# A fused attention and squared-ReLU MLP kernel: one written order for all five engines in place of a scheduled plan

## The chip, the cores and the metric

The kernel runs on one core of a Trainium2 chip. The metric is the device time of one execution in microseconds (us). Three runs of the kernel before gave 272.69 to 273.59 us, with a median of 273.18 us.

## The reference

There are 8 batches (b) of 8 heads, 576 tokens and a head dimension of 64. A second small input `p` has 32 rows per batch and head. All inputs are float32.

```
def sm_attn(qq, kk, vv):                       # softmax attention, scale 1/8
    s = scale * matmul(qq, kk.T); s = s - max(s)
    a = exp(s); a = a / (sum(a) + 1e-9)
    return matmul(a, vv)
p_packed = sm_attn(p, k, v)                    # 32 rows look at 576 tokens
out      = sm_attn(q, p_packed, p_packed)      # 576 tokens look at 32 rows
x = out as (8*576 tokens) x (8 heads*64)       # 4608 x 512
h = x @ w_in                                   # 512 -> 2048
y = square(max(h, 0)) @ w_out                  # 2048 -> 512
```

## The kernel before

**Units.** The heads are taken four at a time (`qd` = 0 or 1), so that 4 heads x 32 rows of `p` fill 128 partitions. For each of the 16 pairs (batch, `qd`) there is an attention chain, written as small steps named `st_...`:

- `st_k`, `st_q` (L170, L176): VectorE turns the loaded `k_b`, `q_b` into `kT`, `qT` in 32x32 blocks.
- `st_s1` (L183): first scores, 4 matmuls of 128x288 against a block-diagonal `pbd`, which VectorE builds (L110). Then `st_max1` (L193) and `st_exp1` (L198).
- `st_e1T` (L217): 6 transposes on TensorE; `st_e1T_out` evicts them; `st_pv` (L229): 24 small matmuls; `st_pp` scales; `st_bd` builds the second block-diagonal `bd`; `st_ppT` (L253).
- `st_s2` (L183): second scores, again 4 matmuls; then `st_turn2` (L265), `st_max2` (L269), `st_sub2` (L273), `st_exp2` (L278), `st_sum2` (L283), `st_a2` (L289), `st_a2T` (L296).
- `st_wp` (L305): the value product is folded into the MLP's first weights, `wp` = packed rows @ `w_in`, in two steps of 8 matmuls, with an eviction `wp<-ps_wp` (L309) each.

**The MLP.** Layer 1 of a batch makes `ps_h` = `wp` x `a2T`, 16 blocks of 128 features in two halves of 288 tokens, two matmuls each (L376; for batch 0 both halves at once, L393). ScalarE applies the ReLU into `r` (L379, L397), VectorE squares `r` into `gT` (L382, L402). Layer 2 makes 36 tiles of 128 tokens, `ps_o` += `gT` x `w_out_bf`, 16 matmuls of 128x512 each (L413). ScalarE evicts each tile into `o_sb` (L423), and four DMAs of 64 KB write it out (L429).

**What sets the order.** `first_batch` and `second_batch` are orders written out by hand for the engines; `busy` puts dummy matmuls (L159) between early steps. From there on `run` builds a plan: each unit of work gets a due time (batch number plus a fraction), for instance

```
at = (-0.12 if b > 2 else None, 0.02, 0.1, 0.18, 0.3, 0.38, 0.48, 0.6, 0.68)
plan.sort(key=lambda x: x[:2])
```

The sorted plan is TensorE's order; the tile scheduler places VectorE, ScalarE, GpSimd and the queues. Loads are issued from GpSimd's queue (`load1`, L129 and L132; `load_w_in`, L117; `load_w_out`, L122); outputs from SP's.

**PSUM.** Eight banks: two double-bank tiles `psa` for the attention steps, and two each of `psh` and `pso` for the MLP's two layers.

Of the kernel before, what the change touches and what calls it, by code (L numbers as in the profile page):

```python
# [17 lines left out]
POOL = mybir.EngineType.Pool  # L18

P = 128  # L20
D = 64
# [7 lines left out]
SCALE = 0.125  # L29


class Kernel:
# [10 lines left out]

    def __init__(self, tc, ctx, q, k, v, p, w_in, w_out, out):
        self.tc, self.nc = tc, tc.nc
        self.q, self.k, self.v, self.p = q, k, v, p
        self.w_in, self.w_out, self.out = w_in, w_out, out
        self.B, self.H = q.shape[0], q.shape[1]
        self.NQ = self.H // QH
        self.DM, self.DFF = w_in.shape  # L50
        self.NE = w_out.shape[1]
        self.NFB = self.DFF // P
        pool = lambda name, bufs: ctx.enter_context(tc.tile_pool(name=name, bufs=bufs))
        psum = lambda name, bufs: ctx.enter_context(
            tc.tile_pool(name=name, bufs=bufs, space=bass.MemoryType.PSUM))
        self.consts = pool("consts", 1)
        self.ld = pool("ld", 3)
        self.tp = pool("tp", 2)
        self.sm = pool("sm", 2)
        self.keep = pool("keep", 4)  # L60
        self.rp = pool("rp", 6)
        self.op = pool("op", 3)
        self.psa = psum("psa", 2)
        self.att = {}
        self.setup()

    def setup(self):
# [6 lines left out]
        make_identity(nc, self.ident)  # L74
# [12 lines left out]

        self.pT = self.consts.tile([P, G, 2 * NP], BF16, name="pT")
        self.pbd = self.consts.tile([P, G, QH, NP, 2], BF16, name="pbd")
# [4 lines left out]
    def p_cast(self):  # L94

        self.tc.keep_in_program_order(
            self.nc.vector.tensor_copy(self.p_b[:, :2 * self.NQ, :], self.p_f))

    def p_turn(self, g0, g1):
        self.tc.keep_in_program_order(  # L100
            self.nc.vector.transpose(self.pT[:, g0:g1, :].bitcast(U32), self.p_b[:, g0:g1, :].bitcast(U32)))

    def pack_diagonal(self, b):
        for g in range(b * self.NQ, (b + 1) * self.NQ):
            self.block_diagonal(self.pbd[:, g, :, :, :], self.pT[:, g, :])
# [8 lines left out]
    def load_w_in(self, c2):  # L114
        for c in range(2):
            f = c * (self.DFF // 2) + c2 * 512
            self.nc.gpsimd.dma_start(  # L117
                self.w_in_bf[c * D:(c + 1) * D, :, c2 * 512:(c2 + 1) * 512],
                self.w_in[:, f:f + 512].rearrange("(h d) f -> d h f", d=D))
# [5 lines left out]
    def load1(self, b, qd, n):  # L125
# [7 lines left out]
        self.att.setdefault((b, qd), {})[n] = x  # L133

    def load_behind(self, b):

        with self.tc.issue_after(self.last_pool):
            for n in "kvq":
                for qd in range(self.NQ):
                    self.load1(b, qd, n)  # L140
        with self.tc.issue_after(self.last_square):
            self.pack_diagonal(b)
# [9 lines left out]
    def psum(self, name, bufs):  # L152
        return self.tc.tile_pool(name=name, bufs=bufs, space=bass.MemoryType.PSUM)

    def busy(self, n):

        ps = self.idle.tile([P, 512], F32, name="ps_idle")
# [3 lines left out]
    def spare32(self, name):  # L161
        return self.spare.tile([P, 512], F32, name=name, tag="s")

    def spare16(self, name):
        return self.spare.tile([P, 1024], BF16, name=name, tag="s")
# [20 lines left out]

    def st_s1(self, t, g):
        t["ps_s1"] = self.turn32("ps_s1")
        self.scores(t["ps_s1"], self.pbd[:, g, :, :, :], t["kT"])
# [23 lines left out]
    def st_e1T(self, t, spare=False):  # L213
        nc = self.nc
        ps = (self.spare16("ps_e1T") if spare else self.turn16("ps_e1T")[:, 0, :])[:PS, :J * P].rearrange("p (j c) -> p j c", c=P)
        for j in range(J):
            nc.tensor.transpose(ps[:, j, :], t["e1"][:, j * PS:(j + 1) * PS], self.ident)  # L217
# [6 lines left out]
    def st_pv(self, t, spare=False):  # L224
        nc = self.nc
        ps = self.spare32("ps_pv")[:, :D] if spare else self.turn32("ps_pv")[:, 0, :D]
# [14 lines left out]
    def st_bd(self, t):  # L241
# [3 lines left out]
        nc.vector.transpose(x[:].bitcast(U32), t["pp"][:, 0, :].bitcast(U32))  # L245
        t["bd"] = self.tp.tile([P, QH, NP, 2], BF16, name="bd")
        self.block_diagonal(t["bd"][:], x[:])

    def st_ppT(self, t, spare=False):

        nc = self.nc
        ps = self.spare16("ps_ppT")[:, :P] if spare else self.turn16("ps_ppT")[:, 0, :P]
        nc.tensor.transpose(ps, t["pp"], self.ident)  # L253
        t["ppT"] = self.keep.tile([P, P], BF16, name="ppT")
        nc.scalar.copy(t["ppT"], ps)

    def st_s2(self, t):
        t["ps_s2"] = self.turn32("ps_s2")
        self.scores(t["ps_s2"], t["bd"][:], t["qT"])
# [16 lines left out]
    def st_exp2(self, t):  # L276
        t["e2"] = self.tp.tile([P, T, NP], F32, name="e2")
        self.nc.scalar.activation(t["e2"], t["d2"], ACT.Exp)  # L278
# [8 lines left out]
    def st_a2(self, t, engine):  # L287
        t["a2"] = self.tp.tile([P, T, NP], BF16, name="a2")
        ins = engine.tensor_tensor(out=t["a2"], in0=t["e2"], in1=t["rs"][:, :].unsqueeze(2).to_broadcast([P, T, NP]),  # L289
                                   op=ALU.mult)  # L290
        if engine is self.nc.gpsimd:
            self.last_pool = ins.ins

    def st_a2T(self, t):
        t["a2T"] = self.keep.tile([P, S], BF16, name="a2T")
        self.last_turn = self.nc.vector.transpose(t["a2T"], t["a2"][:].rearrange("p t i -> p (t i)")).ins  # L296

    def st_wp(self, t, qd, c2):
        nc = self.nc
        if c2 == 0:  # L300
            t["wp"] = self.keep.tile([P, 2, self.DFF // 2], BF16, name="wp")
        ps = self.turn32("ps_wp")
        for h in range(QH):
            for c in range(2):
                nc.tensor.matmul(ps[NP * h:NP * h + NP, c, :],  # L305
                                 lhsT=t["ppT"][D * c:D * c + D, NP * h:NP * h + NP],
                                 rhs=self.w_in_bf[D * c:D * c + D, QH * qd + h, c2 * 512:(c2 + 1) * 512],
                                 start=True, stop=True)
        nc.scalar.copy(t["wp"][:, :, c2 * 512:(c2 + 1) * 512], ps)  # L309

    def steps(self, b, qd):

        t, g = self.att[b, qd], b * self.NQ + qd

        dve = self.nc.vector

        pin = self.tc.keep_in_program_order if b < 4 else lambda ins: ins

        def k():
            pin(self.st_k(t))  # L320

        def s1():
            self.st_s1(t, g)
            self.st_max1(t)
            self.st_exp1(t)
            self.st_rden(t)

        def q():
            pin(self.st_q(t))

        def e1T():
            self.st_e1T(t)
            self.st_e1T_out(t, dve)

        def pv():
            self.st_pv(t)
            self.st_pp(t, dve)

        def ppT():
            self.st_bd(t)  # L340
            self.st_ppT(t)

        def s2():
            self.st_s2(t)
            self.st_turn2(t)
            self.st_max2(t)
            self.st_sub2(t, dve)
            self.st_exp2(t)
            self.st_sum2(t)
            self.st_a2(t, dve)  # L350
            self.st_a2T(t)

        return [k, s1, q, e1T, pv, ppT, s2, lambda: self.st_wp(t, qd, 0), lambda: self.st_wp(t, qd, 1)]

    def att_stream(self, b):


        at = (-0.12 if b > 2 else None, 0.02, 0.1, 0.18, 0.3, 0.38, 0.48, 0.6, 0.68)
        return [(0.3 * qd + x, lambda qd=qd, n=n: self.steps(b, qd)[n]())
                for qd in range(self.NQ) for n, x in enumerate(at) if x is not None]  # L360
# [3 lines left out]
    def mlp1_units(self, b, fbs):  # L364
        nc = self.nc
        c0 = (b % 4) * S

        hold = {}

        def unit(fb, hf):  # L370
            if hf == 0:
                hold[fb] = self.rp.tile([P, S], BF16, name="r")
            ps = self.psh.tile([P, 512], F32, name="ps_h")[:, :HALF]
            for qd in range(self.NQ):
                t = self.att[b, qd]
                nc.tensor.matmul(ps, lhsT=t["wp"][:, fb // (self.NFB // 2), fb % (self.NFB // 2) * P:(fb % (self.NFB // 2) + 1) * P],  # L376
                                 rhs=t["a2T"][:, hf * HALF:(hf + 1) * HALF],
                                 start=(qd == 0), stop=(qd == self.NQ - 1))
            nc.scalar.activation(hold[fb][:, hf * HALF:(hf + 1) * HALF], ps, ACT.Relu)  # L379
            if hf == 1:  # L380
                r = hold.pop(fb)
                self.last_square = nc.vector.tensor_tensor(out=self.gT[:, fb, c0:c0 + S], in0=r, in1=r, op=ALU.mult).ins  # L382

        return [lambda fb=fb, hf=hf: unit(fb, hf) for fb in fbs for hf in range(2)]

    def mlp1_whole(self, b, fb):

        nc, n = self.nc, self.NFB // 2
# [320 lines left out]
```

## Time and profile before

| what | value |
|---|---|
| median of 3 runs | 273.18 us (272.69 to 273.59) |
| the profiled execution: its own time / its span | 272.51 us / 270.7 us |
| granted TensorE clock, mean over the span | 0.992 |
| TensorE busy | 244.8 us (90%) |
| VectorE busy | 186.9 us (69%) |
| ScalarE busy | 170.6 us (63%) |
| GpSimd busy | 40.4 us (15%) |
| moved by DMA | 28.46 MB, of it 18.55 MB by GpSimd's queue |

The profile is one execution. The span runs from the first to the last thing that it recorded; 1.8 us of the execution's time lie around it. A mean duration of an instruction includes a latency that overlaps the next instruction on the same engine, so the distance between two starts is shorter than the mean. The records of 32 of the 576 layer-2 matmuls are missing; all 576 of their weight loads are there. So matmuls are counted here by weight loads (PEld).

### The profile page before, as it was taken

To read this page: it belongs to the slowest core of one execution; us is meant where nothing else is said; L and a number is where in the kernel's file an instruction comes from. 1 tells how busy PE (TensorE), PEld (TensorE's weight loads), DVE (VectorE), ACT (ScalarE), POOL (GpSimd) and SP (SyncE) were. 2 spreads that over 40 slices of the span, in tenths; PEclk is the share of its full clock that TensorE was granted. 3 is DMA by queue.
4 is the path that set the end of the run, shared out by engine and by line. 5 is a ranking of instruction groups with operands and counts; after the bars stand their busy time and mean duration, and the time that the engine had idled before them with its cause. 6 is when DMAs were issued, how large, how long until landed. Compare 5 with 4: busy or idle time off the path is not lost.

```text
span 270.7 us, 5349 instructions
## 1 busy us (share of the span) xinstructions
PE 244.8 (90%) x2003; PEld 136.9 (51%) x2035; DVE 186.9 (69%) x388; ACT 170.6 (63%) x375; POOL 40.4 (15%) x67
## 2 busy tenths in 40 slices
PE   6657778998959999999999999999999999999993
PEld 4424453455415555555556555564555554555441
DVE  3697998777974999868985789579955776333000
ACT  1334857677844777877785687758776678776110
POOL 8445415310101320011001010010000000000000
PEclk9999999999997999999999999999999999999999
DMA  7999999998326797475645481151111211211333
GB/s 114 196 206 199 206 207 208 207 244 143 45 68 99 132 177 122 83 123 90 122 82 89 78 128 42 41 84 41 39 39 44 49 44 44 60 39 39 80 78 78
DMA packets 24249, 28.46 MB, mean 105 GB/s; under 512 B 5280, under 2 KB 15520, under 8 KB 24224
## 3 DMA queue, kind: packets, MB, share of 16 engines
q0 software_dynamic: 16784, 18.55, 43.9%
q1 hardware_dynamic: 7344, 9.45, 14.1%
q8 instruction: 16, 0.26, 0.4%
q10 hardware_dynamic: 96, 0.13, 0.2%
q14 instruction: 9, 0.07, 0.1%
HBM read 37.22 MB, written 9.44 MB: 172 GB/s over the span
## 4 chain that ended last, share of the span: by engine, by line
PE 64%; ACT 12%; DMA 10%; DVE 8%; issue 4%; SPq 1%; POOL 1%; ACTq 0%; POOLq 0%
PE ps_o L413 35%; PE ps_h L376 19%; DMA k_b<-in_k_dram 6%; PE ps_s L183 5%; ACT wp L309 4%; ACT r L379 4%; DMA q_b<-in_q_dram 2%; PE ps_wp L305 2%; ACT e L278 2%; PE ps_e1T L217 1%; ACT r L397 1%; DVE qT L176 1%; DMA out_dram<-o_sb 1%; ACT e L198 1%; PE ps_pv L229 1%
## 5 line engine op out<-in xcount | busy, mean ns | idle before, releaser
L413 PE MATMUL ps_o<-w_out_bf,gT 128*128 128x512 bf16 x544 | 160.0, 382 | 1.8 <-ACT r L397 0.5
L379 ACT ACTIVATE r<-ps_h 128x288 bf16<-128x288 f32 x224 | 90.5, 414 | 44.7 <-PE ps_h L376 42.6
L376 PE MATMUL ps_h<-a2T,wp 128*128 128x288 bf16 x448 | 92.1, 287 | 3.3 <-ACT r L379 1.8
L382 DVE TENSOR_TENSOR gT<-r 128x576 bf16<-128x576 bf16 x112 | 50.3, 450 | 41.8 <-ACT r L379 41.2
L413 PEld LDWEIGHTS <-gT 128*128 128x128 bf16 x576 | 55.6, 98 | 31.9 <-issue 3.8
L376 PEld LDWEIGHTS <-wp 128*128 128x128 bf16 x448 | 43.4, 98 | 48.9 <-issue 9.5
L309 ACT CAST wp<-ps_wp 128x1024 bf16<-128x1024 f32 x32 | 32.3, 1013 | 6.8 <-PE ps_wp L305 6.0
L423 ACT COPY o_sb<-ps_o 128x512 f32<-128x512 f32 x35 | 20.6, 593 | 12.5 <-PE ps_o L413 6.6
L198 ACT ACTIVATE e<-ps_s,nm 128x576 bf16<-128x576 f32 x16 | 11.9, 743 | 14.1 <-DVE nm L193 14.1
L170 DVE STREAM_TRANSPOSE kT<-k_b 128x576 uint32<-128x576 uint32 x16 | 15.0, 946 | 3.8 <-DMA k_b<-in_k_dram 3.6
L129 POOL DMA_DIRECT2D v_b<-in_v_dram x16 | 11.0, 690 | 39.8 <-PE ps_pv L229 36.0
L305 PE MATMUL ps_wp<-w_in_bf,ppT 64*32 64x512 bf16 x256 | 13.3, 386 | 3.8 <-DMA w_in_bf<-in_moe_w_in_dram 2.9
L183 PE MATMUL ps_s<-kT,pbd 128*128 128x288 bf16 x64 | 10.8, 289 | 5.8 <-DVE kT L170 5.8
L397 ACT ACTIVATE r<-ps_h 128x576 bf16<-128x576 f32 x16 | 10.2, 657 | 7.9 <-PE ps_h L393 7.4
L283 DVE TENSOR_REDUCE sums<-e 128x18 f32<-128x576 f32 x16 | 11.9, 746 | 4.6 <-ACT e L278 4.5
L132 POOL DMA_DIRECT2D k_b<-in_k_dram x16 | 8.8, 550 | 39.7 <-DVE kT L170 17.1
L132 POOL DMA_DIRECT2D q_b<-in_q_dram x16 | 8.7, 543 | 40.0 <-DVE qT L176 39.2
L193 DVE TENSOR_REDUCE nm<-ps_s 128x1 f32<-128x576 f32 x16 | 11.9, 743 | 2.3 <-PE ps_s L183 2.0
L265 DVE STREAM_TRANSPOSE s<-ps_s 128x576 f32<-128x576 f32 x16 | 12.4, 778 | 1.2 <-PE ps_s L183 0.6
L278 ACT ACTIVATE e<-d 128x576 f32<-128x576 f32 x16 | 10.9, 683 | 3.5 <-DVE d L273 1.8
L183 PE MATMUL ps_s<-qT,bd 128*128 128x288 bf16 x64 | 10.8, 289 | 2.2 <-DVE qT L176 2.0
L176 DVE STREAM_TRANSPOSE qT<-q_b 128x576 uint32<-128x576 uint32 x16 | 12.2, 762 | 0.3 <-DMA q_b<-in_q_dram 0.3
(48 smaller groups left out, 192.3 us busy)
## 6 DMA issues: line engine op xcount, KB each, us to landing
out_dram<-o_sb SPq DMA_DIRECT2D x142, 64.0 KB, 1.7
k_b<-in_k_dram POOLq DMA_DIRECT2D x16, 288.0 KB, 5.4
q_b<-in_q_dram POOLq DMA_DIRECT2D x16, 288.0 KB, 5.8
v_b<-in_v_dram POOLq DMA_DIRECT2D x16, 288.0 KB, 6.2
w_in_bf<-in_moe_w_in_dram POOLq DMA_DIRECT2D x4, 512.0 KB, 14.3
w_out_bf<-in_moe_w_out_dram POOLq DMA_DIRECT2D x4, 512.0 KB, 13.9
p_b<-in_p_dram POOLq DMA_DIRECT2D x1, 192.0 KB, 15.9
p_f<-in_p_dram SPq DMA_DIRECT2D x1, 128.0 KB, 2.2
```

Of the source, the lines that this page charges most:

```text
L132: self.nc.gpsimd.dma_start(x, s.rearrange("h (l t) d -> (h l) t d", t=T))
L170: return self.nc.vector.transpose(t["kT"][:].rearrange("p (j l a) e -> p a j l e", j=J, a=3).bitcast(U32).rearrange("p a j l e -> p a j (l ...
L176: return self.nc.vector.transpose(t["qT"][:].rearrange("p s e -> p (s e)").bitcast(U32), t["q"][:].rearrange("p t d -> p (t d)").bitcast(U32))
L183: self.nc.tensor.matmul(ps[:, hf, :HALF], lhsT=bd[:, :, e], rhs=x[:, hf * HALF:(hf + 1) * HALF, e], start=(e == 0), stop=(e == 1))
L278: self.nc.scalar.activation(t["e2"], t["d2"], ACT.Exp)
L305: nc.tensor.matmul(ps[NP * h:NP * h + NP, c, :], lhsT=t["ppT"][D * c:D * c + D, NP * h:NP * h + NP], rhs=self.w_in_bf[D * c:D * c + D, QH ...
L309: nc.scalar.copy(t["wp"][:, :, c2 * 512:(c2 + 1) * 512], ps)
L376: nc.tensor.matmul(ps, lhsT=t["wp"][:, fb // (self.NFB // 2), fb % (self.NFB // 2) * P:(fb % (self.NFB // 2) + 1) * P], rhs=t["a2T"][:, hf ...
L379: nc.scalar.activation(hold[fb][:, hf * HALF:(hf + 1) * HALF], ps, ACT.Relu)
L382: self.last_square = nc.vector.tensor_tensor(out=self.gT[:, fb, c0:c0 + S], in0=r, in1=r, op=ALU.mult).ins
L413: nc.tensor.matmul(hold[tt], lhsT=self.gT[:, fb, a:a + P], rhs=self.w_out_bf[:, fb, :], start=(fb == 0), stop=(fb == self.NFB - 1))
L423: nc.scalar.copy(o, ps)
```

## The change

The due times, the hand-written first two batches and the scheduler's part are gone. One text, `ORDER`, lists some 1,400 steps, and every engine, SP's queue included, takes its instructions in that order.

A word is a step: `L` a load (`Lk01` is `k` of batch 0, `qd` 1), `Wi`/`Wo` a quarter of `w_in`/`w_out`, `Z` dummy matmuls. `kT s1 m1 x1 rd eT eo pv pp bd qT pt po s2 t2 m2 sb x2 su a2 aT w0 W0 w1 W1` are the attention steps in the order of the list above, the capital `W` being the eviction of `wp`; `D` builds one `pbd`. `h` is a piece of layer 1 (`h1.0.8`: batch 1, half 0, block 8), `r` its ReLU, `q` a square, `o` two matmuls of layer 2 (`o2.0`: tile 2, first pair), `c` the eviction of a tile. After a colon stands the engine: `v` VectorE, `a` ScalarE, `p` GpSimd.

- Evictions (`eo pp po W r c`) go to VectorE or ScalarE word by word. Of the ReLUs 177 of 240 are on ScalarE, of the 36 tile evictions 26; 9 are on VectorE, and the last is split between both, as before.
- Tiles 0 to 3 of layer 2 (`EARLY`) are summed side by side in four PSUM banks, over the feature quarters 0, 2, 1, 3; the extra two banks (`early`) are given to `psh` when tiles 0 and 1 are evicted.
- For batches 0 to 2 (`DIAG`) the scores are 16 matmuls of 32x288 on the diagonal 32x32 tiles of the array, straight from `pT` or `ppd`, and no block-diagonal operand is built.
- `a2` is written with pairs of tokens interleaved, so that `a2T` is turned as 288 four-byte elements in place of 576 two-byte ones; an output tile goes out in two DMAs of 128 KB (the last tile in four of 64 KB).
- A square takes two blocks of one half (2 x 288) in place of one block of 576.

```diff
+ORDER = """
+Lk00 P1 Lk01 kT00 P0 kT01 I Z25 s100 Lq01 m100 Z5 s101 Lk10 m101 x101 Lv01 Z10 eT01 kT10 eo01:v rd01 Lk11 x100 rd00
+Z4 pv01 pp01:a eT00 qT01 bd01 Z2 s201 kT11 eo00:a t201 Lv00 Lq00 Z3 s111 m111 pv00 pp00:a bd00 pt01 x111 qT00 m201
+Wi00 Wi01 po01:v Z9 s200 t200 Wi11 pt00 s110 po00:a Wi10 m200 sb01:p Lq11 m110 sb00:p x201 Z15 w000 su01 x200 x110
+W000:a su00 a201:p w001 eT11 a200:v Lv11 aT01 W001:a aT00 h0.11 h0.9 eo11:a r0.11:v eT10 rd11 q0.11 h0.3 w101 r0.9:a
...
+    STAGES = ((("spare", 3), ("idle", 1)), (("pair", 2),), (("pso", 2), ("early", 2)), (("psh", 2),))
...
+    def diagonal_scores(self, ps, x, y):
+        x = x.rearrange("p (i e) -> p i e", e=2)
+        for hf in range(2):
+            for e in range(2):
+                for h in range(QH):
+                    c = slice(NP * h, NP * h + NP)
+                    self.nc.tensor.matmul(ps[c, hf, :HALF], lhsT=x[c, :, e],
+                                          rhs=y[c, hf * HALF:(hf + 1) * HALF, e],
+                                          start=(e == 0), stop=(e == 1))
...
+    def relu(self, engine, r, ps):
+        if engine is self.nc.scalar:
+            engine.activation(r, ps, ACT.Relu)
+        else:
+            engine.tensor_scalar_max(r, ps, 0.0)
...
+            fb = QUARTERS[i // n] * n + i % n if tt < EARLY else i
...
+    def run(self):
+        with self.tc.manual_schedule(engines={PE, DVE, ACTE, POOL, SP}):
+            for word in ORDER.split():
+                self.step(word)
```

## The prediction

> **What bounds the kernel now.** I read the shares and slices first, then the starts of TensorE's work, then the chain for unit costs.
>
> ```profile
> PE 244.8 (90%) x2003; PEld 136.9 (51%) x2035; DVE 186.9 (69%) x388; ACT 170.6 (63%) x375; POOL 40.4 (15%) x67
> PE   6657778998959999999999999999999999999993
> DMA  7999999998326797475645481151111211211333
> ```
>
> From slice 14 on TensorE is full; before, it is not, while DMA is. TensorE's timeline shows the holes:
>
> ```profile
> 16.35 0.37 PE L305 MATMUL ps_wp<-w_in_bf,ppT 64*32 64x512 bf16 x1 [0.22 <-DMA w_in_bf<-in_moe_w_in_dram]
> 19.40 0.62 PE L305 MATMUL ps_wp<-w_in_bf,ppT 64*32 64x512 bf16 x15 [2.68 <-DMA w_in_bf<-in_moe_w_in_dram]
> 42.88 1.89 PE L413 MATMUL ps_o<-w_out_bf,gT 128*128 128x512 bf16 x7 [0.47 <-ACT r L397]
> 81.18 0.68 PE L183 MATMUL ps_s<-kT,pbd 128*128 128x288 bf16 x4 [2.96 <-DVE kT L170]
> ```
>
> Layer 2 starts at 42.88. At 78.2 TensorE stands 3 us behind the first scores of batch 3, whose `kT` sits on VectorE behind the last steps of batch 2; the granted clock is 0.5 for 3.4 us after that. The chain of waits gives steady unit times:
>
> ```profile
> 247.19 0.24 PE ps_h L376 x2
> 52.33 0.51 PE ps_s L183 x4
> 248.79 8.20 PE ps_o L413 x38
> ```
>
> So a layer-2 matmul is 8.20/38 = 0.216 us, layer 1 0.122, a score set 0.512. Six `e1T` take 0.336 (starts 0.056 apart). Eight `ps_wp` are bracketed by `ps_o` starts at 193.25 and 193.90: 0.65 less 0.216 = 0.434. Twenty-four `ps_pv` likewise:
>
> ```profile
> 89.35 0.38 PE L413 MATMUL ps_o<-w_out_bf,gT 128*128 128x512 bf16 x1
> 89.66 0.36 PE L229 MATMUL ps_pv<-v_b,e1T 96*32 96x64 bf16 x24
> 89.95 0.39 PE L413 MATMUL ps_o<-w_out_bf,gT 128*128 128x512 bf16 x1
> ```
>
> 0.60 less 0.216 = 0.385. TensorE's work in all: 576 x 0.216 + 512 x 0.122 + 32 x 0.512 + 32 x 0.434 + 16 x (0.385 + 0.336 + 0.056) = 124.4 + 62.5 + 16.4 + 13.9 + 12.4 = 229.6 us. Its last matmul ends at 266.3, so 36.7 us are lost, and 4.4 follow (two half evictions, the last DMAs). Weight loads counted by stretch place the loss:
>
> - 0 to 42.9: work 16.7, lost 26.2
> - 42.9 to 52.7 (layer 1 of batch 1 starts): work 9.4, lost 0.4
> - 52.7 to 90: work 30.5, lost 6.8
> - 90 to 266.3: work 173.0, lost 3.3
>
> The change leaves this work as it is, so its worth is what it does to the 36.7.
>
> **Part 1: start to the first layer-2 matmul.** Up to `o2.0` the order holds the same work plus one `w` set, 17.2 us. What paces it is the load queue. A `k`, `q` or `v` is 288 KB, a quarter of `w_in` or `w_out` 512 KB; slices 3 to 9 move about 205 GB/s: 1.44 and 2.56 us. Before, six attention loads and two `w_in` quarters make 13.8 us, and that second quarter was in at 19.4: add 5.6. (Check: two more quarters and a `k` make 20.3 + 5.6 = 25.9, where `kT` of batch 1 started.) Now eight attention loads precede `w_in`: the second quarter is in at 16.6 + 5.6 = 22.2, the fourth at 27.4, then `q11` 28.8, `v11` 30.3, `v10` 31.7, `k20` 33.1, `q10` 34.6, `Wo0` 37.1, `Wo2` 39.7, `Wo1` and `Wo3` 43.2 and 45.8. On GpSimd's queue `Lq11` stands behind `sb01:p` (1.2 us, waits for `m201`, about 18); the queue then still has bytes until 27.4, so this costs nothing; without that cover it would be about 1.5.
> `w000` can start at 22.2; two `w` sets and two evictions of 1.0 bring `h0.11` to about 25 (23.3 before, with waits of 1.1 and 1.2 later). `aT00` fits: `q00` in at 17.1, then qT 0.76, scores 0.6, t2 0.78, m2 0.73, `sb` on GpSimd 1.2, exp 0.68, sums 1.0, `a2` 0.8 and `aT` 0.5 end near 24.5. After three `h` TensorE waits for `w101` until 27.4, the whole of layer 1 queued behind it. Thirteen blocks remain at the pace of ScalarE's ReLU (L397, 0.60 each of a pair of 1.19) plus `W100`, 1.0: 37.3; `s210` needs `q10` and its turn; with `w010` the first `o` is at 38.4. Bounds: 37.1 (`Wo0`) and 42.9 (nothing gained). Lost: 21.2.
>
> **Part 2: first `o` to the first `h1`.** 13.5 us of work. The first 15 pairs of matmuls (6.5 us) use only quarters 0 and 2, of which `Wo2` is in at 39.7; the first that needs `Wo1` (43.2) comes after 45, so no load is late. Handing the `early` banks to `psh` adds a wait: `h1.0.8`, with all of TensorE's queue behind it, needs `c1:v`. Between `o1.7` and `h1.0.8` stand 1.4 us of matmuls; an eviction of 128x512 on VectorE is not in this trace, at 128x256 it is 0.42 and at 576 wide 0.74, so 0.7 plus 0.3 to start: hidden; uncovered 1.0. I take 0.6 lost (0.4 before).
>
> **Part 3: first `h1` to first `h2`.** 24.0 us of work; 25 ReLUs, 3 evictions and the chain make 24.1 us on ScalarE and 23.9 on VectorE by mean durations, some 20 and 20 by start distances (ReLU pairs follow 0.33 apart). That is tight; I take 1.5 lost, 0.5 to 5 as bounds. The waits of 52.7 to 90 have their place here: second scores now stand 12 us of matmul work or more ahead of the layer 1 that needs them (the steps from `t2` to `aT` sum to 5.7), and from batch 3 on each `kT` stands ahead of the `aT` of the batch before it. What is late next is ScalarE.
>
> **Part 4: the rest.** 174.9 us. Per batch VectorE 27 to 30 us by means (about 24 by distances) against TensorE's 28.6; ScalarE 19 to 22. Removed from VectorE: 12 builds of `pbd` or `bd` at 0.415 = 5.0; `aT` at half the elements, between rows of 128, 384 and 576 elements (0.31, 0.56, 0.76) 0.47 for 0.77: 16 x 0.30 = 4.8. Added: 60 ReLUs of 128x288 from PSUM on VectorE, absent from the trace: 0.34 (128x128, L239) below, 0.74 (576) above; I take 0.46, by the 256-wide row. `a2` with interleaved writing: 0.81 as now, or up to 1.44 (the one at 20.98, beside a GpSimd step). All this is beside TensorE. I take 3.6 lost, next to 3.3 of the last stretch; bounds 1.5 and 9.
>
> **Diagonal scores.** Four rounds of four concurrent matmuls: 4 x 0.128, plus the two changes of array tiling that bracket `pv` above (0.60 - 0.216 - 0.29 = 0.09 before it and about 0.10 after): 0.70 for 0.51. Twelve sets; eight lie in part 1 beside waits (nothing; uncovered 1.5), four in parts 2 and 3: 0.8 us. Concurrency is not in the trace for this shape; the ends are these 0.8 and one at a time, 16 x 0.128 = 2.05 a set. I take the first, as the 24 `pv`, six rounds on four column strips, start 0.29 us in all.
> The Trainium skill speaks against this step ("TensorE: Matmul & The Clock Gate", Part 3, what overlaps): a weight load passes a running matmul only where the row groups differ, and each round returns to the groups of the round before. By that rule three loads of 0.098 stand bare per set, some 3.5 us over twelve. This trace disagrees for `pv`: 24 loads of 0.097 on the same row groups would take 2.3 us, and 0.29 were seen.
>
> **Sum.** 38.4 + (13.5 + 0.6) + (24.0 + 1.5) + (174.9 + 3.6) + 0.8 = 257.3; tail 4.4 (the same halves and four DMAs; half as many output issues on SP earlier, off the path): span 261.7, with 1.8 around it 263.5 against the profiled 272.51. The median of the runs, 273.18, lies 0.67 above that execution; I leave this in the range.
>
> **Rivals.**
> (a) The loads keep the start as long: first `o` at 42.9. For it: DMA share at 9 until slice 9, and later `w_in`. Against: ahead of `w_out` stand the same bytes but for one `k` more, and the wait that ends at 42.88 is a ReLU's, not a load's. Time 263.5 + 4.5 = 268.
> (b) Slower: the fixed order blocks at the heads of queues. Each `h` has two `psh` banks, so it waits for the ReLU two before; that ReLU stands on ScalarE or VectorE behind an attention step that itself waits. There are 224 such `h`; 10 us come from one stall of 0.7 (one VectorE step) at every 16th. Against: 0.9 us is needed from one `h` to the next but one, and the order mostly leaves 1.2. Price at 8% of the 212 us behind the first `o`: 17.0 lost there in place of 0.6 + 1.5 + 3.6 = 5.7, so 263.5 + 11.3 = 274.8. It decides from 9.8 us more than forecast.
> (c) Diagonal matmuls run one at a time: 1.54 more for twelve sets, 18.5; four wholly on the path, half of the rest: 12.3 - 0.8, so 275. Against: the `pv` row.
>
> **How the numbers follow.** Forecast 0.68; (a) 0.15; (b) 0.10; (c) 0.03; the gain eaten by stalls of 8 to 10 us, no change, 0.04. A measurement of this kernel tells 0.3% (0.8 us) from no change. Faster 0.83, same 0.04, slower 0.13. Low end: 37.1 at the first `o` and 3 us less lost after it, 258 (under it 0.07). High end: (a) with 4 us more lost, 272 (over it 0.13).
>
> **What would show it.** The first `ps_o` near 38.4 and the first `ps_h` of batch 1 near 52.5; no wait of 3 us at the first scores of a batch; the clock whole from there; 16 diagonal matmuls starting within 0.5 us. Wrong if ReLU releases many waits of TensorE after 60 us, or VectorE exceeds 90% of a stretch.

## The result, and the profile after

The changed kernel takes 260.31 us (median of 4 runs, 259.61 to 261.81) against 273.38 us for the kernel before in the same rounds (272.69 to 274.66). The ratio is 0.9524, with a 95% interval of 0.9465 to 0.9583: 4.8% faster. The forecast was 263.5 us, with a range of 258 to 272. The profiled execution took 260.88 us, its span is 259.1 us.

Engines, slices and clock, from the page of the kernel after (columns as on the page before):

```profile
span 259.1 us, 5533 instructions
PE 244.5 (94%) x2152; PEld 136.6 (53%) x2185; DVE 201.6 (78%) x439; ACT 146.9 (57%) x313; POOL 42.6 (16%) x69
PE   8767999999999999999999999999999999999991
PEclk9999799999999999999999999999999999999999
```

TensorE reads 9 in every slice from the fifth on (from 26 us), where before it did so from the thirteenth on (from 81 us). VectorE does more (the ReLUs), ScalarE less. The busy time of TensorE is nearly the same (244.5 us for 244.8): its holes have shrunk. Its timeline at the two marks of the prediction, the first layer-2 matmul and the first layer-1 piece of batch 1:

```profile
39.54 0.41 PE L438 MATMUL ps_wp<-w_in_bf,ppT 64*32 64x512 bf16 x8
39.88 2.33 PE L506 MATMUL ps_o<-w_out_bf,gT 128*128 128x512 bf16 x9
...
53.36 0.69 PE L308 MATMUL ps_s<-kT,pT 32*32 32x288 bf16 x16
53.98 0.66 PE L454 MATMUL ps_h<-a2T,wp 128*128 128x288 bf16 x4
```

The waits of TensorE in the stretch from 53.9 us to its last matmul, before (from its own mark, 52.6) and after (waiter, who was waited for: us in total, times, the longest). Before, the two largest of four:

```profile
PE ps_s L183 <- DVE kT L170: 3.0, 1, 3.0
PE ps_h L376 <- ACT r L379: 1.8, 5, 0.8
```

After, the whole answer:

```profile
PE ps_o L506 <- issue: 0.3, 2, 0.2
```

So behind the first 54 us no wait of TensorE for another engine is listed any more. The same sums by stretch as in the prediction, with weight loads counted and a set of diagonal scores put at its measured 0.615 us (time lost = length less work). The mark of batch 2 is the weight load of layer 1 that comes 64 such loads behind the mark of batch 1. In the change, where two batches overlap a little, it lies 0.1 us behind the first layer-1 matmul of batch 2, at 78.54:

| stretch | before: lost | after: from, to | after: lost | forecast: to | forecast: lost |
|---|---|---|---|---|---|
| start to first layer 2 | 26.2 | 0, 39.9 | 21.9 | 38.4 | 21.2 |
| to layer 1 of batch 1 | 0.4 | 39.9, 54.0 | 0.4 | 52.5 | 0.6 |
| to layer 1 of batch 2 | 5.4 | 54.0, 78.7 | 0.25 | 78.0 | 1.5 |
| to the last matmul | 4.8 | 78.7, 253.7 | 0.3 | 256.5 (257.3 with the scores) | 3.6 |
| behind it | 4.4 | 253.7, 259.1 | 5.4 | 261.7 | 4.4 |

(For before, this mark lies at 82.4.)

### The profile page after: what moved, and what is told of

The parts are those of the page before. It is cut to its first block, busy times and chain, and to the rows that moved or that the text cites. A ratio compares the mean times of both kernels' runs of the same rounds, so it can differ in the third digit from the quotient of the medians.

```text
span 259.1 us, 5533 instructions
## 1 busy us (share of the span) xinstructions
PE 244.5 (94%) x2152; PEld 136.6 (53%) x2185; DVE 201.6 (78%) x439; ACT 146.9 (57%) x313; POOL 42.6 (16%) x69
## 4 chain that ended last, share of the span: by engine, by line
PE 82%; DMA 6%; DVE 6%; POOL 2%; issue 1%; ACT 1%; SPq 0%; ACTq 0%; POOLq 0%
PE ps_o L506 44%; PE ps_h L454 26%; PE ps_s L297 4%; DMA q_b<-in_q_dram 4%; PE ps_wp L438 4%; PE ps_e1T L344 2%; DMA k_b<-in_k_dram 2%; PE ps_pv L356 2%; PE ps_s L308 1%; POOL d L408 1%; DVE gT L495 1%; DMA out_dram<-o_sb 1%; DVE mx L404 1%; DVE kT L284 1%; DVE sums L418 1%
## 5 line engine op out<-in xcount | busy, mean ns | idle before, releaser
L506 PE MATMUL ps_o<-w_out_bf,gT 128*128 128x512 bf16 x543 | 145.0, 379 | 1.8 <-issue 0.5
L460 ACT ACTIVATE r<-ps_h 128x288 bf16<-128x288 f32 (+1 forms) x177 | 72.7, 430 | 64.3 <-PE ps_h L454 59.2
L454 PE MATMUL ps_h<-a2T,wp 128*128 128x288 bf16 x512 | 93.9, 289 | 1.2 <-DVE a2T L432 0.5
L454 PEld LDWEIGHTS <-wp 128*128 128x128 bf16 x512 | 47.4, 98 | 41.8 <-issue 5.9
L495 DVE TENSOR_TENSOR gT<-r 128x576 bf16<-128x576 bf16 x128 | 54.7, 450 | 4.1 <-ACT r L460 3.9
L462 DVE TENSOR_SCALAR r<-ps_h 128x288 bf16<-128x288 f32 (+1 forms) x63 | 29.3, 468 | 20.5 <-PE ps_h L454 19.6
L337 ACT CAST wp<-ps_wp 128x1024 bf16<-128x1024 f32 x30 | 30.2, 1013 | 5.3 <-PE ps_wp L438 5.2
L337 ACT COPY o_sb<-ps_o 128x512 f32<-128x512 f32 x26 | 15.2, 584 | 15.5 <-PE ps_o L506 15.4
L268 PE MATMUL ps_idle<-nought 128*128 128x288 bf16 x73 | 12.4, 326 | 1.1 <-DVE nought L182 1.1
L404 DVE TENSOR_REDUCE mx<-s 128x18 f32<-128x576 f32 x16 | 11.8, 740 | 0.1
```

Source lines behind the costliest of these rows:

```text
L268: self.nc.tensor.matmul(ps[:, :HALF], lhsT=self.nought[:, :P], rhs=self.nought, start=True, stop=True)
L337: engine.copy(out, x)
L404: self.nc.vector.tensor_reduce(out=t["mx"], in_=t["s2"], op=ALU.max, axis=AX.X)
L454: self.nc.tensor.matmul(ps, lhsT=t["wp"][:, fb // n, fb % n * P:(fb % n + 1) * P], rhs=t["a2T"][:, hf * HALF:(hf + 1) * HALF], start=(qd = ...
L460: engine.activation(r, ps, ACT.Relu)
L462: engine.tensor_scalar_max(r, ps, 0.0)
```

## Experiments

Times are medians; all are to be read beside the kernel before of the same rounds (272.1, 272.4, 273.0 and 272.2 us in the four groups).

**The changed kernel once more (e0).**

> The changed kernel itself, for comparison on the same chip: 259.5 to 262.

Measured: 259.66 us (259.48 to 260.35), ratio 0.9544 [0.9517, 0.9571]. First layer 2 at 39.55, lost behind 53.65 again 0.25 and 0.31 us.

**The hole at 78 us, in the kernel before (b1).**

```diff
-        return [(0.3 * qd + x, ...
+        f = 0.75 if b == 2 else 1
+        return [(f * (0.3 * qd + x), ...
```

> The kernel before, with one edit: the due times of the attention steps of batch 2 are pressed together to three quarters, so that its chain ends sooner. Theory A (the 3 us hole at 78 us and the half clock behind it come from a chain placed too late): the hole shrinks or goes, TensorE loses 2 to 5 us less between 52.7 and 90; 268.5 to 271.5. Theory E (VectorE and ScalarE are too full there to run the chain sooner): the hole moves or stays, 272 to 274.

Measured: 267.91 us (267.82 to 268.73), ratio 0.9839 [0.9811, 0.9867], 4.5 us less than before. The same scores in its TensorE timeline:

```profile
78.20 0.69 PE L183 MATMUL ps_s<-kT,pbd 128*128 128x288 bf16 x4 [0.43 <-DVE kT L170]
```

The wait of 2.96 us is 0.43, and the half clock behind it is gone too (no drop between 23 us and the last matmul). The mark of batch 2 is at 79.4 for 82.4; 2.8 us less are lost ahead of it and 1.6 us less behind it. Theory A holds, and the time lies 0.6 us under its range: one chain was due too late. In the order written out for the whole kernel this wait is gone as well.

**All ReLUs on ScalarE (e1).** Every `r...:v` of the order becomes `r...:a`.

> All 63 ReLUs that the order gives to VectorE go to ScalarE; nothing else moves. Theory A (the order itself keeps TensorE fed: chains stand far ahead, pieces of layer 1 stand apart): ScalarE's load per batch grows by some 8 x 0.41 = 3.3 us to about 23 to 25 of TensorE's 28, so little is lost, 260 to 263 us, and TensorE's loss after the first layer-1 matmul of batch 1 stays under 3 us (0.8 with the split). Theory B (the split of the ReLUs over two engines is what removed the 3.3 us that were lost after 90 us before): that loss comes back, 4 us or more, and the wait of layer 1 for ScalarE's ReLU is again the longest of TensorE's waits, 264 us or more.

Measured: 263.05 us (262.91 to 263.23), ratio 0.9662 [0.9634, 0.9691], 3.4 us more than e0. Lost: 0.9 us to layer 1 of batch 2 and 2.9 behind it, for 0.25 and 0.31. Neither expectation is met in full: the time lies just above the range of A, and the 3.8 us lost lie between A's 3 and B's 4. As B expected, ScalarE's ReLU is again TensorE's longest wait. The whole list of TensorE's waits behind 53.7 us:

```profile
PE ps_h L454 <- ACT r L460: 1.3, 3, 0.7
PE ps_h L454 <- ACT wp L337: 0.3, 2, 0.2
```

The longest of them, on TensorE and then on ScalarE:

```profile
142.81 0.41 PE L454 MATMUL ps_h<-a2T,wp 128*128 128x288 bf16 x2
143.96 0.40 PE L454 MATMUL ps_h<-a2T,wp 128*128 128x288 bf16 x2 [0.74 <-ACT r L460]
143.01 0.58 ACT L337 COPY o_sb<-ps_o 128x512 f32<-128x512 f32 x1 [0.84 <-PE ps_o L506]
143.49 0.72 ACT L460 ACTIVATE r<-ps_h 128x288 bf16<-128x288 f32 x2
```

These are the words `c15:a bd50 r4.0.10:v ... h4.0.5 r4.0.5:a h4.0.6` of the order. In the change VectorE takes the ReLU `r4.0.10`; in e1 it stands on ScalarE behind the eviction `c15`, which waits for its tile's last matmul, and `h4.0.6` needs the bank that this ReLU frees. Counted from the trace, eight pieces of layer 1 behind 53.7 us start late, 3.0 us in all, each 0.05 us after the end of a ReLU (six) or of an eviction of `wp` (two) on ScalarE. ScalarE is not full (106.1 of the 150 us from 90 to 240): it is late at these places, not overloaded. VectorE's squares also wait longer for ScalarE's ReLUs (27.2 us behind 53.7 us, for 3.5 in the change), but no wait of TensorE for VectorE is listed there. That is rival (b) of the prediction, seen at a price of 3.4 us.

**The split alone, in the kernel before (b2).**

```diff
-            nc.scalar.activation(hold[fb][:, ...], ps, ACT.Relu)
+            if (2 * fb + hf) % 4 == 1:
+                nc.vector.tensor_scalar_max(hold[fb][:, ...], ps, 0.0)
+            else:
+                nc.scalar.activation(hold[fb][:, ...], ps, ACT.Relu)
```

> The kernel before, with one edit: of the ReLUs from batch 1 on every fourth goes to VectorE (56 of 224), about as many as in the changed kernel. Theory A (the split alone is worth little, the order is the gain): 272 to 274, and TensorE loses about 3 us after 90 us as before. Theory B (the split removed that loss): TensorE loses under 1 us after 90 us; 270 to 271. Theory F: VectorE, fuller by 56 x 0.45 = 25 us, holds up squares and chains, 274 or more.

Measured: 273.74 us (271.54 to 275.93 in 10 runs), ratio 1.0037 [1.0006, 1.0067]. The 3.0 us wait for `kT` is there unchanged, the mark of batch 2 is at 85.0 for 82.4, and behind it 4.4 us are lost for 4.8. Theory A: the split is worth nothing by itself. With e1: the split is worth its 3.4 us only under the new order.

**Block-diagonal operands again (e2).** `DIAG = 0`, and the words `D00` to `D21` put in ahead of the scores.

> Batches 0 to 2 use the block-diagonal operand again, its 12 builds put on VectorE just ahead of the scores. Theory A: a set of scores gets 0.11 us shorter on TensorE (0.51 for 0.62), which is worth 0.4 us for the four sets after the first layer-2 matmul, while in the start four builds of 0.42 us stand on the chain from the first load to the second scores; the first layer-2 matmul comes 0.5 to 1.5 us later; 260.5 to 262. Theory C (the diagonal tiles give no gain; the changes of array tiling cost what the builds cost): within 0.5 us of the changed kernel, first layer-2 matmul within 0.3 us of 39.9.

Measured: 259.84 us (258.80 to 260.27), ratio 0.9540 [0.9509, 0.9572], beside 259.66 for e0. First layer 2 at 39.36, for 39.55 in e0 of the same rounds (and for the 39.9 that the expectation named). Theory C: no gain of the diagonal scores can be told. The four builds do stand in the start, but there TensorE waits for `w_in` anyway (1.1 us in this profile, 0.17 in that of the change). The two first matmuls of layer 2 are not quite comparable: the profile of e2 has the whole clock there, that of e0 half of it for 3.4 us from 24.9.

**Tiles 0 to 3 one by one (e3).** The 32 `o` words of these tiles are written tile by tile into the same places; `q0.7 q0.14 q0.12 q0.5` move behind `t210`.

> Layer 2 of tiles 0 to 3 is done one tile after the other, in the places where the order has them side by side; four squares move ahead on VectorE for that (1.5 us earlier in its queue). Theory A: tile 0 needs the second and fourth quarter of w_out with its 5th and 7th pair of matmuls, that is 1.7 and 2.6 us after the first; those quarters land at about 43 and 46, the first pair starts at about 40 to 41, so TensorE stands 2 to 4 us in front of w_out, and the first layer-1 piece of batch 1 moves from 54.0 to 56 to 58: 262 to 265. Theory D (the loads have landed by then, the sum side by side gains nothing): no wait for w_out, 260 to 261.5.

Measured: 265.00 us (263.90 to 265.57), ratio 0.9731 [0.9695, 0.9767], 5.3 us more than e0. TensorE's timeline:

```profile
39.25 1.04 PE L506 MATMUL ps_o<-w_out_bf,gT 128*128 128x512 bf16 x4
40.58 1.02 PE L506 MATMUL ps_o<-w_out_bf,gT 128*128 128x512 bf16 x4 [0.29 <-DMA w_out_bf<-in_moe_w_out_dram]
44.36 1.01 PE L506 MATMUL ps_o<-w_out_bf,gT 128*128 128x512 bf16 x2 [2.75 <-DMA w_out_bf<-in_moe_w_out_dram]
45.30 0.63 PE L438 MATMUL ps_wp<-w_in_bf,ppT 64*32 64x512 bf16 x8
45.86 4.94 PE L506 MATMUL ps_o<-w_out_bf,gT 128*128 128x512 bf16 x12
```

The waits are those expected (0.29 + 2.75), but layer 1 of batch 1 comes 5.7 us later, at 59.3, for 56 to 58. The rest is the clock: it is granted at 0.5 from 43.3 on for 6.8 us (length, busy time of PE, PEld, DVE, ACT and POOL, then PEclk, DMA share, GB/s), and twelve matmuls take 4.9 us where the steady 0.216 makes 2.6:

```profile
43.30:50.13 6.83, 5.77 (x20) 1.64 (x20) 2.90 (x5) 1.59 (x2) 2.76 (x4) 0.50 1.08 186
```

The sum side by side over quarters in the order of their loads is worth these 5.3 us: without it the new start hits `w_out`.

**The start: load of q first (i1), dummy matmuls (i2), later `w101` and `w100` (j1), more bytes (j2).**

i1 moves `Lk11` behind `Lq00` and the steps of that unit behind `s200` (the loads of `w_in` and `sb01` move up with this, and `po01` goes to ScalarE); i2 writes `w000 Z5 ... w001 Z3 eT11 Z3`; j1 is i1 with the whole last tile (below) and

```diff
-... q0.11 h0.3 w101 r0.9:a h0.1 q0.9 eo10:a W101:v r0.3:a w100 rd10 h0.10 Lv10 r0.1:a r0.10:v q0.3 W100:a h0.8 ...
+... q0.11 h0.3 r0.9:a h0.1 q0.9 eo10:a r0.3:a rd10 h0.10 Lv10 r0.1:a r0.10:v q0.3 w101 W101:v h0.8 w100 ...
```

> The changed kernel with the load of k of the second unit of batch 1 moved behind v and q of the first unit of batch 0; the steps of that unit of batch 1 move behind the second scores of batch 0. Theory A (the start is paced by the loads): q lands 1.4 us sooner, the second scores of batch 0 start at about 17.2 for 18.6, and the first layer 1 at 24.6 for 25.6, where w_in and its evictions hold it; the first layer-2 matmul 0.3 to 1 us sooner; 259.5 to 260.5. Theory G (the start is paced by ScalarE's evictions and ReLUs and the last quarter of w_in): first layer-2 matmul unmoved within 0.3 us.

> The changed kernel with 11 more dummy matmuls in TensorE's waits between 22 and 25.6 us. Theory A: the clock stays whole at 26 to 29.4 us; layer 1 of batch 0 loses 0.5 to 1 us less at its start, the first layer-2 matmul comes 0 to 0.8 us sooner. Theory G: that stretch waits for w_in and ReLUs anyway, so no gain although the clock is whole; first layer-2 matmul within 0.2 us.

> The changed kernel with the load of q first, the last tile evicted whole, and the two steps that need the last quarter of w_in moved three and two blocks of layer 1 later. No dummy matmuls are added. Theory K (the start is paced by the landing of the last quarter of w_in: in the five runs of this order with their profiles so far the first layer-2 matmul came 10.8 to 12.1 us after the step w101, and that step waited for this load): three blocks of layer 1 run in front of the wait, the first layer-2 matmul comes 0.5 to 1.5 us sooner than 38.9, the time is 257 to 258.5. Theory G (ScalarE's ReLUs and evictions pace it): first layer-2 matmul at 38.5 to 39.5 as with the load of q first alone, 258 to 259.

> The changed kernel with two more loads (288 and 192 KB, read by nothing) ahead of the first quarter of w_in; all else as it was. At 205 GB/s they take 1.44 + 0.96 = 2.4 us of the load queue. Theory K (the load queue paces the start): w101 and the first layer-2 matmul come 1.8 to 2.6 us later, 262 to 262.7 us. Theory G (ScalarE's work paces it): 0 to 0.8 us later, 259.7 to 260.5.

| run | time, us | layer 1 of batch 0 | `w101` | first layer 2 | half clock from |
|---|---|---|---|---|---|
| change | 260.31 | 25.6 | 28.9 | 39.9 | 26.0 |
| e0 (change) | 259.66 | 25.5 | 28.8 | 39.6 | 24.9 |
| i1 | 259.51 (258.83 to 260.29) | 24.9 | 28.2 | 38.9 | none |
| i2 | 259.67 (258.88 to 260.06) | 24.9 | 28.4 | 39.2 | none |
| j1 | 259.35 (258.58 to 260.07) | 25.0 | 29.8 | 40.0 | 24.8 |
| j2 | 261.76 (261.27 to 262.50) | 26.6 | 30.1 | 40.9 | 23.0 (for 6.8 us, the others 3.4) |

j2: 2.1 us more than e0 for 2.4 us more bytes, and in its profile TensorE stands for the second quarter of `w_in`:

```profile
24.21 1.05 PE L439 MATMUL ps_wp<-w_in_bf,ppT 64*32 64x512 bf16 x15 [2.06 <-DMA w_in_bf<-in_moe_w_in_dram]
```

So the load queue does pace the start (theory K), though its profile shows only 1.0 to 1.3 us of the 2.1 at the first layer 2, and its longer half clock has an unmeasured part in that. The other way round nothing is gained, and j1's time is in neither of its two expected ranges: i1's second scores come at 17.1 for 18.6 and layer 1 0.7 us sooner, as expected, and then TensorE waits 1.13 us for the last quarter of `w_in`; j1 moves that step away and waits 0.71 us for its eviction instead. Loads and ScalarE's chain stand within about a microsecond of each other. i2 kept the clock whole and moved the first layer 2 by 0.4 to 0.7 us; the times of i1, i2 and e0 do not tell. Three profiles share one start word for word: the change, e0 and i3 below. In them the clock drops at 26.0, 24.9 and 8.1 us, and the first layer 2 comes at 39.9, 39.55 and 39.2. So a drop between 23 and 29 us goes with 0.4 to 0.7 us there; what makes it fall at one place or another in the same order stays open.

**The tail (i3, and all together in i4).**

```diff
-        if last:
-            nc.scalar.copy(o[:, :h], ps[:, :h])
-            nc.vector.tensor_copy(o[:, h:], ps[:, h:])
+        self.copy(engine, o, ps)
...
-            for eng, c in ((nc.scalar, slice(0, h)), (nc.sync, slice(h, 2 * h))) if last else ...
+            eng = nc.scalar if last and n else nc.sync
```

> The changed kernel with the last tile evicted whole by ScalarE and written by two DMAs of 128 KB, one from ScalarE's and one from SP's queue, in place of two half evictions and four DMAs of 64 KB. After the last matmul 5.4 us follow now (4.5 before the change). Theory H (the halves are evicted one after the other, 0.37 and 0.42 for 0.59 whole, and four DMAs of shorter pieces cost more to issue and to land): 4.3 to 4.9 us follow, 0.5 to 1.1 us gained. Theory J: the tail is the landing of the last bytes alone, unchanged within 0.2.

> The three edits together: load of q first, more dummy matmuls, last tile whole. If each does what the first theory of each says, 0.8 to 2.9 us less than the changed kernel: 257.5 to 259.5. If only the tail's edit does, 259 to 260.

Measured: i3 258.69 us (258.27 to 259.15), ratio 0.9483 [0.9448, 0.9517]; i4 259.17 us (258.60 to 261.15), ratio 0.9493 [0.9454, 0.9531]. ScalarE's and its queue's rows at the end, of the change and then of i3:

```profile
253.71 0.37 ACT L516 COPY o_sb<-ps_o 128x256 f32<-128x256 f32 x1 [2.82 <-DMA out_dram<-o_sb]
254.12 1.29 ACTq L526 DMA_DIRECT2D out_dram<-o_sb  x2
```

```profile
253.02 0.58 ACT L337 COPY o_sb<-ps_o 128x512 f32<-128x512 f32 x1 [2.82 <-DMA out_dram<-o_sb]
253.64 0.66 ACTq L522 DMA_DIRECT2D out_dram<-o_sb  x1
```

In the change two DMAs of 64 KB take 1.29 us to issue, in i3 one of 128 KB takes 0.66. Behind the last matmul 4.4 us follow in i3, 4.5 in i4 and 4.5 in j1, against 4.8 to 5.5 in the eight profiles with the tail of the change (change, e0, e1, e2, e3, i1, i2, j2). Theory H, by 0.3 to 1.1 us; eviction and DMAs were changed together, so their shares are not told apart. i4 took nothing more from its two edits of the start: its first layer 2 is at 40.7, behind a wait of 1.68 us for `w_in` and a half clock from 29.2. So i3 has the lowest median of all versions run, 0.8 us under i1 and 1.0 under i2 of the same rounds; its interval overlaps that of the changed kernel.

## Why the prediction was right

- **What bounds the kernel.** Shown. TensorE's work is all but unchanged (229.6 us, and 230.8 with the diagonal sets) and the gain is in its holes: lost before its last matmul 36.7 us before, 22.9 after. Of the 13.8 us, 4.3 lie in the start, 5.1 up to the mark of batch 2 and 4.5 behind it. For the last two b1, e1 and b2 are the evidence. What brings the 4.3 us in the start was not taken apart: no run has the new order of loads in the kernel before, and the interleaved `a2` and the larger output DMAs have no run of their own.
- **Part 1, start.** Forecast 38.4 for the first layer 2, measured 39.9 (39.2 to 39.9 in the three profiles of the same start). Up to `w101` the path was about the one told: the second quarter of `w_in` forecast at 22.2, waited for until 22.5; layer 1 forecast at 25, started at 25.6, when both evictions of `wp` (25.4) and the last `aT` (25.5, forecast 24.5) were through. The term that was off is `w101`: 27.4 forecast for the last quarter, 28.2 to 28.6 where the waits in e2, i1 and i4 show its landing, 28.9 in the profile of the change, where the half clock from 26.0 delays the blocks ahead of it. From `w101` to the first layer 2 the forecast had 11.0 us, and 11.0 were measured, but that is luck. The terms it names, 13 x 0.60 and 1.0 behind 27.4, end at 36.2 and not at 37.3, and ScalarE did not set the pace: TensorE's own work there is 9.8 us by the unit times, and ScalarE waited 1.9 us for it, TensorE 0.19 us for ScalarE (28.87 to 39.88):

```profile
ACT r L460 <- PE ps_h L454: 1.9, 6, 0.5
```

- **Part 2.** 14.1 us forecast, 14.1 measured. The wait for `c1:v` was hidden; an eviction of 128x512 on VectorE takes 0.69 us (0.7 taken). That no load is late holds only because of the side-by-side order, as e3 shows: its tile-by-tile order waits 3 us.
- **Part 3.** 25.5 forecast, 24.6 measured (53.98 to 78.54); lost about 0.25 for 1.5. That the hole of before came from a late chain is shown by b1, in the kernel before.
- **Part 4, the mis-sized term.** 3.6 us lost were taken "next to 3.3 of the last stretch"; 0.3 were measured. The step carried over the loss of an order that the change abolishes. The trace before had the reason in it, though its list of waits shows only 0.3 us: behind 90 us, 15 pieces of layer 1 start 0.07 to 0.27 us late, 2.6 us in all, each 0.05 us after the end of the ReLU two before it. One of them, 0.27 late, on TensorE and then on ScalarE, where an eviction of `wp` holds up the ReLU:

```profile
127.54 0.38 PE L413 MATMUL ps_o<-w_out_bf,gT 128*128 128x512 bf16 x1
128.02 0.41 PE L376 MATMUL ps_h<-a2T,wp 128*128 128x288 bf16 x2
126.67 0.99 ACT L309 CAST wp<-ps_wp 128x1024 bf16<-128x1024 f32 x1
127.56 0.71 ACT L379 ACTIVATE r<-ps_h 128x288 bf16<-128x288 f32 x2
```

The new order keeps such pieces apart and gives every fourth ReLU to VectorE. Without the split it loses 3.4 us (e1), and b2 shows that the split alone is worth nothing.

- **Prices that the trace did not show.** ReLU of 128x288 on VectorE 0.454 us (0.46 taken), interleaved `a2` 0.79 (0.81), `aT` 0.447 (0.47), all well placed.
- **Diagonal scores.** A set takes 0.62 us from its first matmul to the next instruction's (0.70 taken, 0.51 before): four rounds of 0.128 and 0.11. So four sets cost 0.4 us, not 0.8. The rule of the Trainium skill ("TensorE: Matmul & The Clock Gate", Part 3) would have left, by an estimate, three weight loads of 0.098 bare per set, 0.29 us beyond the rounds and the change of tiling, which the 0.62 leaves no room for; here too the measurement decides.
- **Tail.** 4.4 forecast ("the same halves and four DMAs"), 5.4 measured in this execution, 4.8 to 5.5 over the eight. The four DMAs are not the same: each is now written in pieces of half a row (1 KB), 64 in place of 32. i3 shows 0.3 to 1.1 us of it.
- **Sum.** +1.5 (start) + 0 - 0.9 (part 3) - 4.2 (part 4 with the 0.8 for the scores: 179.3 forecast, 175.1 measured) + 1.0 (tail) = -2.6: from 261.7 forecast to the span of 259.1. Misses of both signs cancel in part.
- **Rivals.** (a) did not happen: the first layer 2 moved by 3.0 us. (b) did not happen in this order, and e1 is how it looks when one placement is changed under a fixed order. (c) is excluded by the 0.62 us.
- **A sign of being wrong that was met.** VectorE does exceed 90% of a stretch: it is busy 13.38 of the 14.10 us of part 2, 95%, and TensorE loses only 0.4 there. The busy share alone was no sign of a stall.

```profile
39.88:53.98 14.10, 13.75 (x112) 5.98 (x107) 13.38 (x23) 6.32 (x9) 6.25 (x8) 1.00 1.18 197
```

## What to carry to other kernels

Count the bound engine's work by stretch and ask of each lost microsecond what placed it there; a chain that was due a few microseconds too late cost here its wait of 3.0 us and then the half clock behind it (4.5 us in all, b1). A written order and its engine assignment are one thing: the order without its split lost 3.4 us (e1), the split without its order gained nothing (b2). When an order changes throughout, do not carry over the waits of the old one: size them from the distances in the new. And compare each stretch of a forecast with the bound engine's own work in it: a right length can stand on a wrong bound, as from `w101` to the first layer 2.

## What the runs showed of the hardware

- In e3 TensorE waited 2.75 us (to 44.36), and the granted clock was 0.5 from 43.3 on for 6.83 us. In the kernel before it waited 2.96 us (to 81.18), and the clock was 0.5 from 82.3 on for 3.41 us. Matmuls of 128x512 then started 0.43 us apart for 0.216. In e3 that nearly doubled the price of the wait. A wait of 2.68 us in the kernel before (to 19.40) was followed by no half clock, so the length of a wait alone does not tell.
- DMA issue followed the number of pieces here, not the bytes: on ScalarE's queue two DMAs of 64 KB took 0.86 us to issue in rows of 2 KB (before, 32 rows each), 1.29 in rows of 1 KB (change, 64 rows each), and one of 128 KB in rows of 2 KB 0.66 (i3, 64 rows).
- Behind the first layer 2, profiles of the same order lose the same: 0.43, 0.25 and 0.30 to 0.31 us in the three stretches, in seven kernels that differ only in their start and tail. What differs from profile to profile lies in the first 40 us and behind the last matmul.
